# Attention by random features with two feed-forward layers: values by features a slot later, and the first casts on GpSimd

## Chip, cores and metric

The kernel runs on one core of a Trainium2 chip. The metric is the time on the device in microseconds, as the median of three runs. The profile is of one execution of its own.

## What is computed

Attention with positive random features, then a gated feed-forward layer, then one with h cos(h):

```python
def phi(x):
    proj = np.einsum('bhsd,md->bhsm', x, omega)
    h = proj - np.sum(x * x, axis=-1, keepdims=True) / 2.0
    return np.exp(h - np.max(h, axis=-1, keepdims=True)) / np.sqrt(m)
q_p, k_p = (phi(q_s), phi(k_s))          # q, k scaled by D ** -0.25
kv = np.einsum('bhsm,bhsd->bhmd', k_p, v)
z = np.sum(k_p, axis=2)
x = einsum(q_p, kv) / (einsum(q_p, z) + 1e-06)
xn = x / rms(x) * rms_g
g = xn @ w_gate
y = (silu(g) * (xn @ w_val)) @ w_out
h = y @ w_in
out = (h * np.cos(h)) @ w_out2
```

There are 4 batches, 8 heads, 576 positions of 64, and 128 features; so 2304 tokens of 512. The inner widths are 1536 and 2048. All is float32.

## The kernel before

The tokens are cut into 18 tiles of 128, of keys and of queries. The attention starts in 24 slots. In each slot one tile, of keys or of queries, is projected on the features (`project`, TensorE, two banks of the ring of four "w" banks), reduced to its maxima (`features`, L435, VectorE) and exponentiated (L437, ScalarE, eight instructions). Slots 0 to 5 are key tiles 0 to 5; then queries 0 to 5 stand in slots 6, 9, 12, 15, 20 and 23, and keys in the others (the last in 21 and 22). The older tiles of queries take further steps in later slots: transposing their features, sums and quotients, the square, its root on GpSimd, the norm (`norm`, L494), turning (`turn`, one "w" bank) and splitting into two parts (`put`, L516 and L518). A key tile's features are multiplied with its values in `kv_product` (L591) one slot after it was projected; tiles 4 and 13 lie in two batches and take two. The values of the tile three later are loaded one slot behind that.

The order is written out by hand: every engine runs its instructions in the order of the program, slot by slot, and within a slot by the line of `older` steps with `begin` in it. The norm comes ahead of the projection, the values by features last.

Between the slots the weights are made ready, 512 columns at a time (a chunk): they come packed, are unpacked by integer operations and split into an upper and a lower part. `wts.tick(n)` does n steps of the generator `run` at the end of a slot. `front` is the unpacking: shift L190 on VectorE (reads W, which `exponent` made on ScalarE), L193 for every third chunk, L195, the `exponent` of the next chunk, L204 on VectorE, L209 on GpSimd. `early_back` of the chunk before is woven in, a step each behind the first two: `high` (L214, a cast on ScalarE, followed by the DMA issue L170 of a chunk three later) and `low` (L217, GpSimd). So step 8c of the count is L190 of chunk c, 8c+1 `high` of chunk c-1, 8c+3 its `low`, 8c+4 L195, 8c+5 the exponent of chunk c+1, 8c+6 L204 and 8c+7 L209. W has one buffer. 25 steps lie in slots 1 to 5, 8 in slots 6 to 13, and 36 in slots 14 to 22.

Behind the slots come 24 steps of the first products (two half steps each; a product and a part of L886), among which the other 12 tiles of queries and the later steps of the weights (`wts.pace`) lie. The rest is products of the later groups and the second layer.

Of the kernel before, what the change touches and what calls it, by code (L numbers as in the profile page):

```python
# [33 lines left out]
F32 = mybir.dt.float32  # L34
# [10 lines left out]
P = 128  # L45
NB = 384
# [10 lines left out]
def attention_then_ffn(ctx: ExitStack, tc: tile.TileContext, qT, kT, v, omT, wc1, rms_g, wc2, out, B, H, S, D):  # L57
    nc = tc.nc
    M = omT.shape[1]
    DM = H * D  # L60
    KD = DM // P
    HP = H // 2
# [21 lines left out]
    def parts(t):  # L84

        pr, i = divmod(t, TPP)
        if i == MIX:
            return [(2 * pr, 0, P // 2), (2 * pr + 1, P // 2, P // 2)]
        return [(2 * pr + (i > MIX), 0, P)]
# [37 lines left out]
    class Weights:  # L127
# [83 lines left out]
            yield  # L211

        def high(self, src, t, to):
            nc.scalar.copy(t[:, 0, to], src)  # L214

        def low(self, src, t, to):
            nc.gpsimd.tensor_tensor(t[:, 1, to], src, f32(t[:, 0, to]), op=ALU.subtract)  # L217
# [184 lines left out]
    wts = Weights()  # L402
# [144 lines left out]
    with tc.manual_schedule():  # L547
        fp = ctx.enter_context(tc.tile_pool(name="fp", bufs=2, reuse_waits="tile"))
        early = ExitStack()
        ap = early.enter_context(tc.tile_pool(name="att", bufs=2, side="right", reuse_waits="tile"))  # L550
        depth = {"gain": 1, "raw": 3, "feat": 3, "mx": 6, "den": 4}
        with_keys = {"raw": 1, "feat": 2}
        turn_of = {"raw": 0, "feat": 0}
        keys = [True]

        def att_tile(what, shape, dt, name):
            own = depth.get(what, 2)
            if keys[0] and what in with_keys:
                n = turn_of[what] % (own + with_keys[what])
                turn_of[what] += 1  # L560
                if n >= own:
                    return vp.tile(shape, dt, tag=what, name=name, bufs=with_keys[what])
            return ap.tile(shape, dt, tag=what, name=name, bufs=own)

        kv = [ap.tile([P, KVW], F32, name=f"kv{b}", bufs=1) for b in range(B)]
        NV = 3
        values = ExitStack()
        vp = values.enter_context(tc.tile_pool(name="values", bufs=1, side="right", reuse_waits="tile"))
        vt = [vp.tile([P, H, D + 1], F32, name=f"v{i}", bufs=1) for i in range(NV)]
        att = Attention(att_tile, "q", kv)  # L570


        acc = {}

        def load_v(t):
            if t < NTILE:
                nc.sync.dma_start(vt[t % NV][:, :, 0:D], v[t])

        def kv_product(t, i):
# [3 lines left out]
            for r in range(2):  # L583
# [3 lines left out]
                for h in range(HP):  # L587
                    hh = 2 * h + r
                    for c in range(2):
                        half_c = slice(c * M // 2, (c + 1) * M // 2)  # L590
                        nc.tensor.matmul(  # L591
                            acc[b, r][half_c, h * P:h * P + D + 1], att.e["k", t, r][p0:p0 + n, h, half_c],
                            vt[t % NV][p0:p0 + n, hh, :],
                            start=begin and h == 0, stop=end, skip_group_check=True)
# [24 lines left out]
        def combinations(p):  # L619
# [27 lines left out]
            for kk in range(2):  # L647
# [19 lines left out]
                less(s3, s3, s1)  # L667
                yield from [None] * (5 if few else 1)
                high(s1)
                yield  # L670
                if few:
                    high(s2)
                    yield from [None] * 4
                lower(s1)
                yield
                if not few:
                    high(s2)
                    yield
# [64 lines left out]
        SLOTS = len(tiles)  # L743
# [3 lines left out]
        begins, then = {}, {}  # L747
        for s, (nm, t) in tiles.items():
            if nm == "k":
                for i in range(len(parts(t))):  # L750
                    then.setdefault(s + 1 + i, []).append((1, kv_product, t, i))
                then.setdefault(s + 2 + i, []).append((0, load_v, t + NV))
            else:
                for i in range(1, 8):
                    at = s + i + (s >= SLOTS - 1 or i > 1)
                    then.setdefault(at, []).append((-i, query_step, t, i))
# [6 lines left out]
        def load_ahead(s):  # L763
            at = order.index(s) if s in tiles else -1
            if at >= 0 and at + AHEAD[0] < len(order) and at + AHEAD[0] not in asked:
                asked.add(at + AHEAD[0])
                att.load(*tiles[order[at + AHEAD[0]]])

        def older(s, *steps):
            for step in steps:  # L770
                for k, f, *args in then.get(s, []):
                    if k == step:
                        f(*args)

        def begin(s):
            if s in tiles:
                att.project(*tiles[s])
                for r in range(2):
                    att.features(*tiles[s], r)
# [21 lines left out]

        for s in range(SLOTS):
            load_ahead(s)
            if s in (0, 1):
                load_v(s + 1)
                wts.load(s + 1, nc.sync)
            if s == 3:
                att.load_gain()
            older(s, 0, -5)
            begin(s)  # L810
            older(s, -7, -6, -4, -3, -1, -2, 1)
            if s:
                wts.tick(5 if s < 6 else 1 if s < 14 else 4 if s + 1 < SLOTS else 0)


        att.tag = "w"
# [48 lines left out]
        def silu(blk, f, ps):  # L865
            a = row(F32, f"gv{blk}_{f}")
            nc.scalar.activation(a, ps, AF.Silu)
            return a
# [82 lines left out]
        for n, (g, blk, f, first, last) in enumerate(steps):  # L951
# [9 lines left out]
            s = SLOTS + 2 * n  # L961
# [3 lines left out]
            a = silu(blk, f, ps)  # L965
# [466 lines left out]
```

## Time and profile before

| | |
|---|---|
| time, median of three runs | 957.8 us (956.14 to 958.7) |
| the profiled execution's own time | 955.29 us |
| its span | 953.5 us |
| TensorE busy | 929.5 us, 97% |
| VectorE busy | 713.4 us, 75% |
| ScalarE busy | 537.1 us, 56% |
| GpSimd busy | 415.5 us, 44% |

The span in 40 slices of 23.8 us, each digit the busy share in tenths; PEclk is the granted clock of TensorE in tenths of full speed:

```profile
PE   8988999999999999999999999999999999999998
DVE  5797777878854685585876658996799787786766
ACT  7898776756535443435363645664655565464443
PEclk9999999989999999999999999999999999999999
```

PE is TensorE, PEld its loading of weights, DVE VectorE, ACT ScalarE, POOL GpSimd, SP SyncE. A line of a timeline gives the start, the duration, the engine, the line of the program, the operation, out<-in, and in brackets how long the engine idled before it and what ended that. Instructions of one engine overlap a little, so what one costs its queue is read from the start of the next rather than from its duration.

### The profile page before, as it was taken

The page shows a single profiled execution, that of the slowest core. Times are in us where ns is not written, and L with a number is a line of the kernel's source. Part 1 is how long each engine was busy: PE and PEld are TensorE (multiplying, and loading weights), DVE is VectorE, ACT ScalarE, POOL GpSimd, SP SyncE. Part 2 cuts the span into 40 slices and gives each one's busy share as a digit, 9 for nine tenths or more (in the row PEclk, how much of TensorE's full clock was granted, in tenths as well). Part 3 has the DMA queues.
Part 4 walks back from the last instruction along what each step waited for, and adds up shares of the span by engine and source line. Part 5 has one row for each costly group of instructions (what it writes and reads, how often), then busy time and mean ns, then how long its engine had stood idle before and what let it go on. Part 6 is the DMA issues. An engine that isn't in the chain of part 4 may idle for free. (4 is left out here: it accounts for less than half of the span.)

```text
span 953.5 us, 17373 instructions
## 1 busy us (share of the span) xinstructions
PE 929.5 (97%) x6337; PEld 866.7 (91%) x6337; DVE 713.4 (75%) x1159; ACT 537.1 (56%) x1155; POOL 415.5 (44%) x377
## 2 busy tenths in 40 slices
PE   8988999999999999999999999999999999999998
PEld 7777998989999999999999998889888988988997
DVE  5797777878854685585876658996799787786766
ACT  7898776756535443435363645664655565464443
POOL 2143387467836975376583763320343220240000
PEclk9999999989999999999999999999999999999999
DMA  9774378777796988766989693967622767307554
GB/s 290 201 192 164 134 264 292 264 257 271 231 346 226 400 288 294 268 200 202 386 297 383 231 374 130 355 211 251 210 93 101 251 205 285 124 21 282 191 227 160
DMA packets 112214, 227.71 MB, mean 239 GB/s; under 512 B 28160, under 2 KB 63616, under 8 KB 112128
## 3 DMA queue, kind: packets, MB, share of 16 engines
q1 hardware_dynamic: 110832, 222.34, 67.5%
q10 hardware_dynamic: 1296, 4.26, 1.4%
q8 instruction: 50, 0.82, 0.4%
q14 instruction: 36, 0.29, 0.1%
HBM read 156.04 MB, written 70.52 MB: 238 GB/s over the span
## 5 line engine op out<-in xcount | busy, mean ns | idle before, releaser
L1253 PE MATMUL o_ps<-w,o 128*128 128x512 f32 x864 | 226.0, 393 | 0.7 <-DVE o L1056 0.7
L209 POOL TENSOR_TENSOR f<-f,raw 128x512 f32<-128x512 f32 x68 | 94.4, 1388 | 229.2 <-DVE raw L204 199.2
L1253 PEld LDWEIGHTS o_ps<-w,o 128*128 128x128 f32 x864 | 159.7, 188 | 24.5 <-DVE o L1056 1.1
L217 POOL TENSOR_TENSOR w<-b,w 128x512 fp32r<-128x512 f32 x88 | 115.5, 1318 | 137.0 <-ACT w L214 113.7
L833 PE MATMUL gv_ps<-xhl,w 128*128 128x384 f32 x576 | 109.3, 338 | 1.3 <-DVE eT L454 1.1
L833 PEld LDWEIGHTS gv_ps<-xhl,w 128*128 128x128 f32 x576 | 101.6, 190 | 2.4 <-DVE eT L454 1.6
L1152 PE MATMUL y<-t,w 128*128 128x384 f32 x576 | 102.0, 334 | 0.3 <-POOL w L217 0.3
L1152 PEld LDWEIGHTS y<-t,w 128*128 128x128 f32 x576 | 100.0, 188 | 0.6 <-POOL w L217 0.6
L1053 ACT CAST o<-turns 128x384 fp32r<-128x384 f32 x96 | 47.4, 513 | 93.4 <-DVE turns L1234 93.4
L1045 PE MATMUL Xh<-T,w 128*128 128x384 f32 x432 | 87.4, 336 | 1.6 <-ACT h L1198 1.6
L1045 PEld LDWEIGHTS Xh<-T,w 128*128 128x128 f32 x432 | 76.8, 188 | 9.7 <-ACT h L1198 4.1
L1045 PE MATMUL X<-T,w 128*128 128x384 f32 x432 | 80.7, 334 | 0.0
L1045 PEld LDWEIGHTS X<-T,w 128*128 128x128 f32 x432 | 75.4, 188 | 0.0
L214 ACT CAST w<-b 128x512 fp32r<-128x512 f32 x88 | 50.5, 580 | 31.9 <-DVE b L274 24.8
L1056 DVE TENSOR_TENSOR o<-turns,o 128x384 fp32r<-128x384 f32 x96 | 60.0, 639 | 8.5 <-ACT o L1053 8.1
L886 PE MATMUL y_ps<-t,w 128*128 128x384 f32 x288 | 61.8, 350 | 0.3 <-ACT t L873 0.3
L1019 ACT ACTIVATE turns<-turns,half_pi 128x768 f32<-128x768 f32 (+1 forms) x50 | 45.7, 914 | 22.8 <-DVE turns L1223 22.7
L1045 PE MATMUL Yh<-B,w 128*128 128x384 f32 x288 | 58.0, 336 | 0.0
L1223 DVE SCALAR_TENSOR_TENSOR turns<-turns,r 128x768 f32<-128x768 int32 (+1 forms) x50 | 56.4, 1128 | 1.7
L1234 DVE TENSOR_TENSOR turns<-h,turns 128x768 f32<-128x768 f32 (+1 forms) x50 | 55.1, 1101 | 2.5 <-ACT turns L1019 2.5
L190 DVE TENSOR_SCALAR f<-W 128x512 int32<-128x512 int32 x68 | 44.0, 647 | 15.1 <-ACT W L182 6.5
L1045 PEld LDWEIGHTS Yh<-B,w 128*128 128x128 f32 x288 | 51.4, 188 | 4.2 <-ACT h L1198 0.4
(116 smaller groups left out, 1804.6 us busy)
## 6 DMA issues: line engine op xcount, KB each, us to landing
T<-T_dram SPq DMA_DIRECT2D x48, 768.0 KB, 7.1
raw<-wc SPq DMA_DIRECT2D x60, 512.0 KB, 5.1
B<-yh_dram SPq DMA_DIRECT2D x21, 768.0 KB, 5.5
kept<-f SPq DMA_DIRECT2D x56, 256.0 KB, 5.1
b<-kept SPq DMA_DIRECT2D x56, 256.0 KB, 4.8
B<-x_dram SPq DMA_DIRECT2D x15, 768.0 KB, 6.7
x_dram<-xhl SPq DMA_DIRECT2D x12, 768.0 KB, 5.7
s<-x_dram SPq DMA_DIRECT2D x24, 384.0 KB, 5.6
```

What stands on the lines that cost most here:

```text
L209: nc.gpsimd.tensor_tensor(f32(f), f32(f), rest, op=ALU.add)
L214: nc.scalar.copy(t[:, 0, to], src)
L217: nc.gpsimd.tensor_tensor(t[:, 1, to], src, f32(t[:, 0, to]), op=ALU.subtract)
L833: nc.tensor.matmul(o, w[i], x[j], start=n == 0, stop=n == len(terms) - 1)
L886: nc.tensor.matmul(yacc[blk][e], w[:, i, e * P:(e + 1) * P], t[:, j], start=first and i + j == 0, stop=last and j == 1)
L1045: nc.tensor.matmul(o, w[:, i, c + kk * P:c + (kk + 1) * P], x[:, j, kk], start=begin and n == 0, stop=n == 5, skip_group_check=True)
L1053: nc.scalar.copy(t[:, 0], a)
L1056: engine.tensor_tensor(t[:, 1], a, f32(t[:, 0]), op=ALU.subtract)
L1152: nc.tensor.matmul(acc[e], w[:, i, e * P:(e + 1) * P], t[:, j], start=f == fs[0] and i + j == 0, stop=f == fs[-1] and j == 1)
L1223: nc.vector.scalar_tensor_tensor(r, a, -TWO_PI_LO, b, op0=ALU.mult, op1=ALU.add)
L1234: at(mu, lambda: nc.vector.tensor_tensor(r, h, r, op=ALU.mult))
L1253: nc.tensor.matmul(oacc[blk][j], o[:, x, js], w[:, y], start=first and n == 0, stop=last and n == 2)
```

## The change

In the first slots the values are multiplied with the features two slots behind the projection instead of one, and at the latest in slot 23. There are four buffers of values instead of three; the fourth is first loaded in slot 2, and each later load stands a slot later. The features of the slots have eight buffers instead of five, three of them borrowed from the rows of the products. The weights take 4 steps instead of 5 in slots 1 to 5 and 2 instead of 1 in slots 6 to 13, which makes 72 instead of 69. While `early` holds (in the slots), `high` is a copy on GpSimd instead of ScalarE. The load of the gains goes from slot 3 to slot 8.

```diff
         def high(self, src, t, to):
-            nc.scalar.copy(t[:, 0, to], src)
+            if self.early:
+                nc.gpsimd.tensor_copy(t[:, 0, to], src)
+            else:
+                nc.scalar.copy(t[:, 0, to], src)
...
-        with_keys = {"raw": 1, "feat": 2}
+        with_keys, vp_bufs = {"raw": 1, "feat": 5}, {"raw": 1, "feat": 2}
...
+                if n >= own + vp_bufs[what]:
+                    a = fp.tile([P, 2, NB], F32, tag="t", name=name, bufs=3).rearrange("p a c -> p (a c)")
+                    return a[:, 0:HP * M].rearrange("p (h m) -> p h m", m=M)
                 if n >= own:
-                    return vp.tile(shape, dt, tag=what, name=name, bufs=with_keys[what])
+                    return vp.tile(shape, dt, tag=what, name=name, bufs=vp_bufs[what])
...
-        NV = 3
+        NV = 4
...
                 for i in range(len(parts(t))):
-                    then.setdefault(s + 1 + i, []).append((1, kv_product, t, i))
-                then.setdefault(s + 2 + i, []).append((0, load_v, t + NV))
+                    then.setdefault(min(s + 2 + i, SLOTS - 1), []).append((1, kv_product, t, i))
+                then.setdefault(s + 3 + i, []).append((0, load_v, t + NV))
...
             load_ahead(s)
+            if s == 2:
+                load_v(3)
...
-            if s == 3:
+            if s == 8:
                 att.load_gain()
...
-                wts.tick(5 if s < 6 else 1 if s < 14 else 4 if s + 1 < SLOTS else 0)
+                wts.tick(4 if s < 6 else 2 if s < 14 else 4 if s + 1 < SLOTS else 0)
```

## Rows read from the trace of the kernel before

**Rows 1.** Timeline of TensorE, around slot 23 and at 200 us.
```profile
78.94 1.16 PE L426 MATMUL qp_ps<-om,qraw 64*128 64x128 f32 x14 [1.65 <-ACT ke L437]
...
81.00 1.10 PE L591 MATMUL kv_ps<-v,ke 128*64 128x65 f32 x32
82.04 4.43 PE L833 MATMUL gv_ps<-xhl,w 128*128 128x384 f32 x24
...
200.32 0.46 PE L426 MATMUL qp_ps<-om,qraw 64*128 64x128 f32 x2 [1.76 <-issue]
```
**Rows 2.** ScalarE's lines, 7:82 us: busy, mean ns | idle before, its end.
```profile
L437 ACT ACTIVATE ke<-kp_ps,kmx 128x128 f32<-128x128 f32 x144 | 39.4, 407 | 7.7 <-DVE kmx L435 7.7
...
L214 ACT CAST w<-f 128x512 fp32r<-128x512 f32 x8 | 5.2, 645 | 2.8 <-POOL f L209 2.8
```
**Rows 3.** Timeline of VectorE, from the reductions of slot 14 to slot 22.
```profile
47.60 1.29 DVE L435 TENSOR_REDUCE kmx<-kp_ps 128x4 f32<-128x512 f32 x2 [1.09 <-ACT ke L437]
48.80 0.75 DVE L518 TENSOR_TENSOR xhl<-xT_ps,xhl 128x256 fp32r<-128x256 f32 x2
49.47 0.42 DVE L195 TENSOR_SCALAR raw<-f 128x512 int32<-128x512 int32 x1
49.80 0.75 DVE L494 SCALAR_TENSOR_TENSOR x<-x,ms,gain 128x512 f32<-128x512 f32 x1
50.67 1.29 DVE L435 TENSOR_REDUCE qmx<-qp_ps 128x4 f32<-128x512 f32 x2
51.88 0.15 DVE L476 TENSOR_SCALAR den<-num_ps 128x4 f32<-128x4 f32 x1
...
53.36 0.68 DVE L204 SCALAR_TENSOR_TENSOR raw<-raw 128x512 f32<-128x512 uint32 x1
53.95 0.42 DVE L190 TENSOR_SCALAR f<-W 128x512 int32<-128x512 int32 x1
...
55.49 0.68 DVE L454 COPY eT<-eT_ps 128x512 f32<-128x512 f32 x1
56.09 0.68 DVE L193 SCALAR_TENSOR_TENSOR f<-W,f 128x512 int32<-128x512 int32 x1
56.80 1.38 DVE L195 TENSOR_SCALAR raw<-f 128x512 int32<-128x512 int32 x1
...
61.06 1.78 DVE L494 SCALAR_TENSOR_TENSOR x<-x,ms,gain 128x512 f32<-128x512 f32 x1
...
71.70 1.61 DVE L494 SCALAR_TENSOR_TENSOR x<-x,ms,gain 128x512 f32<-128x512 f32 x1
...
75.96 1.27 DVE L435 TENSOR_REDUCE kmx<-kp_ps 128x4 f32<-128x512 f32 x2
```
**Rows 4.** Timeline of ScalarE, slots 13 to 15.
```profile
47.36 0.70 ACT L516 CAST xhl<-xT_ps 128x256 fp32r<-128x256 f32 x2
...
49.20 0.62 ACT L214 CAST w<-f 128x512 fp32r<-128x512 f32 x1
49.72 2.18 ACT L437 ACTIVATE ke<-kp_ps,kmx 128x128 f32<-128x128 f32 x8
51.73 0.74 ACT L184 ACTIVATE W<-raw 128x512 f32<-128x512 f32 x1
52.30 2.24 ACT L437 ACTIVATE qe<-qp_ps,qmx 128x128 f32<-128x128 f32 x8
```
**Rows 5.** GpSimd's casts at line L638, whole span: duration in ns, min/median/max.
```profile
L638 POOL CAST s<-s x16: 496/696/1046, 129.2 to 251.4; 128x384 fp32r<-128x384 f32 x16
```
**Rows 6.** Timeline of GpSimd, beside the norm of 61.06 us.
```profile
60.89 1.41 POOL L209 TENSOR_TENSOR f<-f,raw 128x512 f32<-128x512 f32 x1 [0.57 <-DVE raw L204]
```
**Rows 7.** Timeline of VectorE, L190 in slot 5 and at 199 us.
```profile
24.60 0.79 DVE L190 TENSOR_SCALAR f<-W 128x512 int32<-128x512 int32 x1 [0.87 <-ACT W L182]
...
199.13 0.43 DVE L190 TENSOR_SCALAR f<-W 128x512 int32<-128x512 int32 x1 [3.60 <-ACT W L184]
```
**Rows 8.** A stretch: us, busy (count) of PE, PEld, DVE, ACT, POOL, granted clock, DMA.
```profile
200.00:208.00 8.00, 7.25 (x32) 6.87 (x33) 6.84 (x11) 5.43 (x13) 7.68 (x8) 0.57 0.50 181
```

## The prediction

> **What bounds the kernel now.** I read the slices of the page first: TensorE is busy in nearly all of the 953.5 us except at the start, so only a stage in which TensorE has gaps can pay. The change touches the first 24 slots, from 4 us to the first product at 82.04 us [rows 1]. There I read the waits and the lines of ScalarE, then the timelines of ScalarE and VectorE side by side. ScalarE loses 7.7 us waiting for the reductions of VectorE, and 2.8 us in four of its eight casts L214, which wait for GpSimd's L209 [rows 2]. VectorE shows the opposite: from 47.60 us each of its instructions begins where the one before ends, slot after slot, and so with few breaks to 78 us [rows 3]. So in slots 14 to 22 the last wait to end is VectorE's queue; ScalarE is second, TensorE third.
>
> **How the slots hang together.** Every engine runs in program order. Slot s projects on TensorE, reduces on VectorE (L435), exponentiates on ScalarE (L437), does the older steps, and then the steps of the weights. A chunk has eight steps: shift L190 on VectorE, cast L214 and load of a later chunk, L193 (every third chunk), L217 on GpSimd, L195, the next chunk's exponent (ScalarE), L204, L209 on GpSimd. L190 needs the exponent. From the starts of neighbours [rows 3, 4]: reductions 1.2, exponentials 2.01, exponent 0.57 (its own 0.74), L214 0.52, put(0) with square and copy 1.84, L204 0.59, L190 0.42, L193 0.71, L195 0.33, quotients 1.48, L518 0.67, L454 0.60, norm 0.75.
>
> **Part by part.**
>
> The cast: eight of the twelve first chunks reach L214 in the slots. ScalarE loses 8 x 0.52 = 4.2 us of work and the 2.8 us of waits. The DMA issue behind the cast stays on ScalarE and needs the same L209 (its buffer), but now stands a slot behind it, so the wait isn't inherited. ScalarE isn't what ends last, so I cost this at 0; its cover is VectorE's queue, and if that cover were gone it would be worth up to 7.
>
> GpSimd gets eight casts of 128x512. The nearest row casts 128x384 in 0.50 to 1.05 us, median 0.70 [rows 5]; by width 0.66 to 1.39, I take 0.93, in all 7.4 us. They are not late for any reader: low follows them in the same queue. They hold VectorE up, though: the norm takes 1.78 instead of 0.75 when it meets L209, another 1.61, and L195 1.38 instead of 0.43 [rows 3, 6]. These are 1.03 + 0.86 + 0.95 = 2.8 us in slots 14 to 22, beside ten GpSimd instructions of about 1.41, 14.1 us. With four casts more it is, at that rate, 2.8 x 17.8/14.1 = 3.6 us for the changed kernel; the other end is 0, since GpSimd no longer waits for ScalarE and may finish while VectorE itself waits. I take 1.8, the middle.
>
> The Trainium skill speaks against this part (SBUF — State Buffer, Who interferes with whom): VectorE and GpSimd share a port pair as an exclusive lock, and the later one blocks for the whole instruction. The long norms agree. By that rule alone eight casts could cost 8 x 0.93 = 7.4 us.
>
> The step count: this is the term that decides. With 5 and 1 steps, step 37 (the exponent of chunk 5) was the last of slot 14, and its L190 the third step of slot 15. With 4 and 2, 36 steps are done before slot 14, and every even slot from 14 on does exponent, L204, L209, L190 in this order. So L190 waits for an exponent that stands behind this slot's exponentials, and the next slot's reductions stand behind L190, ScalarE behind those. An even slot, reduction to reduction, becomes 0.65 (first reduction) + 2.01 + 0.74 + 0.42 = 3.8 us. It is 4.6 in slots 14 and 20 (the norm follows L190) and 3.8 + 1.84 = 5.7 in slot 16, whose put(0), square and copy stand ahead of the exponent. The odd ones stay as VectorE makes them: slot 15 1.2 + 1.48 + 0.71 + 0.33 = 3.7; 17 1.2 + 0.67 + 0.33 + 0.75 = 2.95; 21 1.2 + 0.60 + 0.71 + 0.33 = 2.8. Slot 19 is set by the bank that the projection of slot 20 waits for: 0.65 + 1.0 (half of the exponentials) + 1.16 [rows 1] + 0.1 = 2.9. The eight from 14 to 21 sum to 31.1, against 75.96 - 47.60 = 28.4 before [rows 3]: +2.7. The trace of before shows this wait once, in slot 5, where exponent and L190 fell into one slot: L190 stood 0.87 us [rows 7].
>
> The same alignment comes in slots 2 and 4, while fewer steps lie in slots 1 to 5 and eight more in 6 to 13. Worked in the same way these stretches come out even at slot 14 (49.65 against 49.72 for the exponentials); bounds -1 and +1.5.
>
> Values by features a slot later: TensorE no longer stands before the 1.04 us of L591 until ScalarE is done, but the projection behind it needs a bank that the same exponentials release, so little is gained; 0 to -1 in slots 2 to 5, inside the bounds above. At the end the last two key tiles both fall into slot 23: TensorE, which waited 1.65 us there before its projection and did one L591 group of 1.04 us [rows 1], does two behind the same wait: +1.0 ahead of the first product.
>
> Fourth buffer, buffers of features, gain: SyncE issues the same loads in the same order; the load of the fourth values waits for nothing, and gain goes five slots later and is first read in slot 12. Three feature buffers lie in the product rows, which nothing else uses before slot 24. 0, hidden under the slots, at most one issue of about 0.5 us.
>
> Sum for the slots: 2.7 + 1.0 + 1.8 = +5.5, bounds +2 and +8.
>
> Behind the slots: 72 instead of 69 steps are done, so each later step comes up to three earlier. In the kernel before, the exponent of chunk 22 and its L190 fall into one half step; L190 stands 3.60 us, L518 and L872 stand behind it, TensorE waits 1.76 us for their banks, and its granted clock is then 0.57 over 8 us [rows 1, 7, 8]: the level of 1.2 GHz for most of it, 0.43 x 7.25 us busy = 3.1 us lost. Three steps earlier the two lie in different half steps. Without that stall some 1.4 of the 1.76 us go (L872's bank would still come a little late, an estimate) and the 3.1 of clock: -4.5. Two other pairs now share a half step (chunks 15 and 25) and could do the same, so the other end is 0. I take the middle, -2.2.
>
> **Sum.** +5.5 - 2.2 = +3.3 us. The profiled execution is 955.3 with a span of 953.5, 2.5 below the median; a difference carries over unchanged, since behind 90 us TensorE is busy nearly throughout (the slices again): 957.8 + 3.3 = 961.1.
>
> **Rivals.**
> *Faster, by the alignment behind the slots.* The stall at 199 us goes whole (-4.5) and no pair takes its place, while the slots cost under 1.5 us, because GpSimd finishes under VectorE's waits (0 for contention) and the missing casts let the exponent come earlier than I count. For it: L190 after L204 often met a finished exponent in before. Against: the chain reduction, exponentials, exponent, L190 has no slack in even slots. It decides where the first product starts before 83.5 us. 957.8 - 3.5 = 954.3.
> *Slower, by the clock.* With 5 us more in the last slots TensorE idles up to 3 us at a time around slots 16 and 20. A gap of 1.65 us before slot 23 left the granted clock at full (the slices of the page); one of 1.76 us at 200 us was followed by 0.57 [rows 1, 8]. If it falls there, projections, sums and the first products take twice as long, and one such stretch costs up to 3.1 us more: about 964 to 965. By the Trainium skill (TensorE: Matmul & The Clock Gate, Part 1: The HAM clock gate) the low level is what an engine without recent work gets; this trace agrees at 200 us only.
> *Nothing that can be measured*, because the steps are re-ordered by slack that I don't see: 957.8.
>
> **How the numbers follow.** The forecast has 0.50; its own range is 957.5 to 964.5 (slots +2 to +8, behind them -4.5 to 0, not both ends at once), of which 0.20 lies within 0.3% (2.9 us, about what a measurement of this kernel can tell from no change) and 0.30 above. Faster by alignment 0.30 (0.27 below, 0.03 within), clock 0.15, nothing 0.05. So faster 0.27, same 0.28, slower 0.45. The range takes in most of the rivals: 951.5 to 966.
>
> **What would show it.** Right: in even slots from 14 VectorE waits at L190 for the exponent, 1 to 3 us each, longest in slot 16; ScalarE waits for L435 right after; first product at 85 to 89 us; two L591 groups ahead of it; no 3.6 us wait near 200 us. Wrong: first product at or before 82 us, L190 without waits, or ScalarE busy without a break in the slots. Then ScalarE was the bound after all and its 4 to 7 us come through, and the forecast's sign is wrong.

## The result and the profile after

The changed kernel takes 969.3 us (median of four runs, 965.82 to 971.72) against 957.0 us for the kernel before beside it (954.85 to 958.7): a ratio of 1.0127, interval 1.0085 to 1.017. It is slower by 12.4 us, where I had forecast 3.3; 969.3 lies above the range. The profiled execution is the quickest of the four (965.8 us, span 964.0 against 953.5), so the trace shows 10.5 of the 12.4 us.

The page of the changed kernel, its slices (tenths busy, as before):

```profile
span 964.0 us, 17342 instructions
...
PE   8969999999999999999999999999999999999998
...
DVE  4877778888953696577684758986889787786766
ACT  5867776776433534355443646564656564454443
...
PEclk8989999999999999999999999999999999999999
```

Most of the loss is made in the first four slices: ScalarE and VectorE are less busy there than before in the first and the third (for ScalarE in part because its eight casts, 5.2 us [rows 2], are gone), TensorE in the third (6 instead of 8 tenths). VectorE's timeline of the changed kernel (start, duration, in brackets the idle time and what ended it) at the shift L190 and at the reductions that open slots 14, 15 and 22 (L438 was L435):

```profile
16.05 0.72 DVE L190 TENSOR_SCALAR f<-W 128x512 int32<-128x512 int32 x1 [1.60 <-ACT W L182]
22.23 1.54 DVE L190 TENSOR_SCALAR f<-W 128x512 int32<-128x512 int32 x1 [2.13 <-ACT W L184]
...
49.93 1.29 DVE L438 TENSOR_REDUCE kmx<-kp_ps 128x4 f32<-128x512 f32 x2 [0.75 <-ACT ke L440]
54.31 0.50 DVE L190 TENSOR_SCALAR f<-W 128x512 int32<-128x512 int32 x1 [1.83 <-ACT W L184]
54.73 1.75 DVE L497 SCALAR_TENSOR_TENSOR x<-x,ms,gain 128x512 f32<-128x512 f32 x1
56.40 1.28 DVE L438 TENSOR_REDUCE qmx<-qp_ps 128x4 f32<-128x512 f32 x2
65.39 0.54 DVE L190 TENSOR_SCALAR f<-W 128x512 int32<-128x512 int32 x1 [2.78 <-ACT W L182]
80.61 0.57 DVE L190 TENSOR_SCALAR f<-W 128x512 int32<-128x512 int32 x1 [1.11 <-ACT W L184]
84.97 1.28 DVE L438 TENSOR_REDUCE kmx<-kp_ps 128x4 f32<-128x512 f32 x2
89.02 0.43 DVE L190 TENSOR_SCALAR f<-W 128x512 int32<-128x512 int32 x1 [2.17 <-ACT W L182]
```

The unbroken queue of [rows 3] now has a hole in slots 14, 16, 20 and 22 where L190 waits for the exponent; slot 18 alone has none. TensorE of the changed kernel, same columns (L597 was L591, L429 L426, L841 L833):

```profile
29.15 2.23 PE L597 MATMUL kv_ps<-v,ke 64*64 64x65 f32 x64
...
67.94 2.04 PE L429 MATMUL kp_ps<-om,kraw 64*128 64x128 f32 x14 [4.37 <-DVE xhl L521]
...
86.88 1.16 PE L429 MATMUL qp_ps<-om,qraw 64*128 64x128 f32 x14 [1.34 <-DVE raw L204]
88.95 2.04 PE L597 MATMUL kv_ps<-v,ke 128*64 128x65 f32 x64
90.91 4.44 PE L841 MATMUL gv_ps<-xhl,w 128*128 128x384 f32 x24
...
258.15 0.66 PE L507 MATMUL xT_ps<-ident,x 128*128 128x128 f32 x4 [2.11 <-ACT gv L875]
...
643.64 1.32 PE L1053 MATMUL Xh<-T,w 128*128 128x384 f32 x6 [1.40 <-ACT h L1206]
```

The first product stands at 90.91 instead of 82.04 [rows 1]: +8.88. This delay is still +8.73 at the start of the 13th step of the products; at the 15th it is +5.16, because the stall at 199 us [rows 7] is gone; at the end of the steps it is +9.1 again, because of the new gap at 258.15, and at the end of the span +10.54. The windows show the clock (us, busy and count by engine, granted clock, DMA share, GB/s); the kernel before had 1.00 in the first three and 0.72 in the fourth:

```profile
10.00:20.00 10.00, 8.11 (x136) 6.86 (x136) 6.60 (x12) 7.06 (x26) 3.22 (x3) 0.84 1.12 293
20.00:30.00 10.00, 9.63 (x146) 8.30 (x146) 7.83 (x14) 7.71 (x29) 4.53 (x5) 0.82 0.89 260
60.00:70.00 10.00, 5.01 (x66) 4.30 (x67) 6.38 (x13) 6.65 (x22) 3.90 (x5) 0.73 0.43 125
196.00:208.00 12.00, 11.47 (x105) 10.75 (x104) 10.95 (x22) 8.73 (x20) 4.89 (x5) 1.00 0.93 317
256.00:264.00 8.00, 5.89 (x27) 5.85 (x27) 7.28 (x11) 3.19 (x8) 7.73 (x8) 0.79 0.67 218
```

### The profile page after: what moved, and what is told of

The parts are those of the page before. It is cut to its first block, busy times and chain, and to the rows that moved or that the text cites. A ratio compares the mean times of both kernels' runs of the same rounds, so it can differ in the third digit from the quotient of the medians.

```text
span 964.0 us, 17342 instructions
## 1 busy us (share of the span) xinstructions
PE 931.1 (97%) x6337; PEld 869.0 (90%) x6337; DVE 715.3 (74%) x1160; ACT 531.9 (55%) x1147; POOL 419.1 (43%) x385
## 5 line engine op out<-in xcount | busy, mean ns | idle before, releaser
L841 PE MATMUL gv_ps<-xhl,w 128*128 128x384 f32 x576 | 109.2, 338 | 2.0 <-DVE den L479 1.0
L841 PEld LDWEIGHTS gv_ps<-xhl,w 128*128 128x128 f32 x576 | 101.5, 190 | 3.2 <-issue 1.6
L1053 PEld LDWEIGHTS Xh<-T,w 128*128 128x128 f32 x432 | 76.8, 188 | 10.5 <-ACT h L1206 4.8
L217 ACT CAST w<-b 128x512 fp32r<-128x512 f32 x88 | 50.5, 580 | 32.8 <-DVE b L277 25.7
L190 DVE TENSOR_SCALAR f<-W 128x512 int32<-128x512 int32 x68 | 47.0, 692 | 23.6 <-ACT W L182 12.4
L204 DVE SCALAR_TENSOR_TENSOR raw<-raw 128x512 f32<-128x512 uint32 x68 | 54.8, 806 | 0.5
```

The lines of the kernel that those rows point to most:

```text
L204: nc.vector.scalar_tensor_tensor(rest, raw[:, :, 0].bitcast(U32), 2.0 ** -52, rest, op0=ALU.mult, op1=ALU.mult)
L841: nc.tensor.matmul(o, w[i], x[j], start=n == 0, stop=n == len(terms) - 1)
L1053: nc.tensor.matmul(o, w[:, i, c + kk * P:c + (kk + 1) * P], x[:, j, kk], start=begin and n == 0, stop=n == 5, skip_group_check=True)
```

## The experiments

**The step count alone, and a shift of it.** steps_only has the new counts and nothing else; before_36_steps leaves slots 1 to 5 alone and reaches the same 36 steps by three more in slot 13.

```diff
-                wts.tick(5 if s < 6 else 1 if s < 14 else 4 if s + 1 < SLOTS else 0)
+                wts.tick(4 if s < 6 else 2 if s < 14 else 4 if s + 1 < SLOTS else 0)   # steps_only
+                wts.tick(5 if s < 6 else 1 if s < 13 else 4 if s + 1 < SLOTS else 0)   # before_36_steps
```

> The kernel before with the new step counts alone (4 and 2 instead of 5 and 1). Theory A (alignment: the exponent and its L190 fall into one slot, and the reductions stand behind L190): L190 waits 1 to 3 us in slots 2, 4, 14, 16, 20 and 22 as in the changed kernel, the first product comes at 87 to 91 us, the time is 7 to 13 us over before. Theory C (the casts on GpSimd hold VectorE up): no cast is moved here, so within 2 us of before. Theory K (values a slot later leave TensorE idle and its clock falls): values are not moved here, so no stretch of half clock in the first 82 us and within 2 us of before.

Measured: 964.7 us, ratio 1.0105 (1.0085 to 1.0125); first product 88.37 (+6.33).

> The kernel before with three more steps in slot 13 (36 done ahead of slot 14, 5 and 1 otherwise): in slots 14 to 22 the phase of the changed kernel, in slots 1 to 12 that of before. Theory A: the L190 waits come in slots 14, 16, 20 and 22 alone; the first product 4 to 7 us later than in before; time 4 to 9 us over before, or up to 4 less where the half clock at 200 us goes. Theories C and K: within 2 us of before.

Measured: 965.2 us, 1.0105 (1.0087 to 1.0123); first product 89.17 (+7.13). So 36 steps ahead of slot 14 cost as much as all of the new counts; what slots 1 to 5 do makes no difference that the intervals show. Both kernels have 72 steps done at the first product instead of 69, as the changed one has; what that costs without the alignment is measured below (before_72). VectorE and TensorE of steps_only:

```profile
51.84 0.43 DVE L190 TENSOR_SCALAR f<-W 128x512 int32<-128x512 int32 x1 [1.84 <-ACT W L184]
61.85 0.43 DVE L190 TENSOR_SCALAR f<-W 128x512 int32<-128x512 int32 x1 [2.79 <-ACT W L182]
77.73 1.38 DVE L190 TENSOR_SCALAR f<-W 128x512 int32<-128x512 int32 x1 [0.85 <-ACT W L184]
...
67.19 1.92 PE L591 MATMUL kv_ps<-v,ke 64*64 64x65 f32 x32
69.03 1.16 PE L426 MATMUL kp_ps<-om,kraw 64*128 64x128 f32 x16
```

From reduction to reduction, slots 14 to 21 take (us):

| slot | 14 | 15 | 16 | 17 | 18 | 19 | 20 | 21 | sum |
|---|---|---|---|---|---|---|---|---|---|
| worked out | 4.6 | 3.7 | 5.7 | 2.95 | 3.8 | 2.9 | 4.6 | 2.8 | 31.1 |
| steps_only | 5.40 | 3.74 | 5.60 | 3.07 | 5.17 | 3.63 | 5.63 | 2.85 | 35.1 |
| changed kernel | 6.47 | 3.74 | 5.71 | 3.78 | 4.20 | 3.14 | 5.15 | 2.85 | 35.0 |

Slots 15, 16 and 21 are as worked out. In 14 the exponentials begin 1.6 us behind the reduction instead of 0.65, since ScalarE is late there. In 18 nothing waits at L190: VectorE's own queue is the longer chain, with the quotients and a copy of the finished sums of the values (L602) that the working had left out; it takes 4.29 at full clock (steps_filler below). On top the values by features run at the half clock (1.92 instead of about 1.1), and the two copies wait 0.23 and 0.36 us for them. In 20 L190 takes 1.38 instead of 0.42.

**One and two steps instead of three.**

```diff
+                wts.tick(5 if s < 6 else 1 if s < 13 else 2 if s < 14 else 4 if s + 1 < SLOTS else 0)   # 34; with 3: 35
```

> The kernel before with one more step of the weights in slot 13 (34 instead of 33 before slot 14). Theory (what costs is that the exponent and the L190 that reads it fall into one slot, not the number of steps): with 34 the exponent is the third step of an even slot and L190 the second of the next, the reductions of a slot between them, so no wait of over 1 us at L190 in slots 14 to 22, first product 81 to 83.5, median within 3 us of before, though before_36_steps, two steps on, cost 9.7. Rival (each step moved ahead of slot 14 costs its own time, some 3 us): first product 84 to 85, median 957.5 to 960.

Measured: 957.2 us, 1.0022 (1.0009 to 1.0034); first product 84.18.

> The kernel before with two more steps of the weights in slot 13 (35 before slot 14). Theory: the exponent is the second step of an even slot and L190 the first of the next, directly ahead of that slot's work but still behind the exponentials of one slot only; the wait is short (under 1 us), first product 81.5 to 84.5, median within 4 us of before. Rival (each step costs its own time): first product 86 to 87.5, median 960 to 963. If 34 or 35 comes out below before by more than 2 us, it beats both kernels.

Measured: 960.7 us, 1.0056 (1.0037 to 1.0074); first product 86.64. Neither idea is right alone: the waits at L190 are gone in both, as the theory wants (at most 0.47 us from slot 14 on), but the first product is as late as the rival said. The rows show another collision. First L204 on VectorE and `low` on GpSimd of before_34_steps, then the norm of before_35_steps with GpSimd's instructions around it:

```profile
51.08 1.80 DVE L204 SCALAR_TENSOR_TENSOR raw<-raw 128x512 f32<-128x512 uint32 x1
51.05 1.28 POOL L217 TENSOR_TENSOR w<-f,w 128x512 fp32r<-128x512 f32 x1 [0.30 <-ACT w L214]
```
```profile
53.05 1.77 DVE L494 SCALAR_TENSOR_TENSOR x<-x,ms,gain 128x512 f32<-128x512 f32 x1 [0.72 <-POOL ms L490]
50.50 1.27 POOL L217 TENSOR_TENSOR w<-f,w 128x512 fp32r<-128x512 f32 x1 [8.73 <-ACT w L214]
51.86 0.51 POOL L489 TENSOR_SCALAR ms<-ms 128x1 f32<-128x1 f32 x1
52.98 1.29 POOL L209 TENSOR_TENSOR f<-f,raw 128x512 f32<-128x512 f32 x1
```

L204 takes 1.80 instead of 0.68 beside L217; with 35 the root that the norm needs also stands behind L217. The price climbs, in the ratios 0.2, 0.6 and 1.05% for 34, 35 and 36 steps, and only the last one has the long waits at L190. It isn't the price of the phase alone (of which step falls into which slot): with these counts 70, 71 and 72 steps are done at the first product, and one or three steps more in slot 23, with the phase untouched, cost 0.2 and 0.42% (before_70 and before_72 below). By these medians the phase is worth some 0.6% at 36 steps and nothing that can be told at 34.

**The change with the alignment taken out.** all_but_steps is the changed kernel with the old counts (the diff above reversed), after_33_steps with 33 steps ahead of slot 14 in another split:

```diff
-                wts.tick(4 if s < 6 else 2 if s < 14 else 4 if s + 1 < SLOTS else 0)
+                wts.tick(4 if s < 6 else 2 if s < 11 else 1 if s < 14 else 4 if s + 1 < SLOTS else 0)
```

> The changed kernel with the old step counts (5 and 1). Theory A: no L190 wait in slots 14 to 22; the first product at 80 to 84 us; time 953 to 960. Theory C: eight casts stay on GpSimd, so 5 to 12 us over before remain. Theory K: the values stay a slot later, the half clock at 17 us stays, and most of the 12 us too.

Measured: 962.1 us, 1.0077 (1.0057 to 1.0096); no wait at L190 in slots 14 to 22, and still the first product at 91.60.

> The changed kernel with 33 instead of 36 steps done ahead of slot 14 (4, then 2 to slot 10, then 1): the phase of before in slots 14 to 22, everything else as changed. Theory A: the first product 4 to 7 us earlier than in the changed kernel (84 to 87 us), L190 waits only in slots 2 and 4; time 958 to 964. Theory C: casts as in the changed kernel, so 966 to 972 stays. Theory K: 966 to 972 stays, with half clock at 17 and 65 us.

Measured: 962.2 us, 1.0064 (1.0043 to 1.0085); first product 89.03. The new counts are thus worth 5 to 6 us in the changed kernel: the alignment together with three steps more at the first product, since both runs have 69 there. And 6 to 7 us stay that I had not counted. From slot 22 to the first product both take 8.44 us against 6.08 before: here the two groups of L591 in slot 23 do cost, part of them at the half clock (3.19 us in all_but_steps).

**The other two parts alone.** casts_only is the kernel before with `high` on GpSimd in the slots; values_only the changed kernel with the old counts and the cast back on ScalarE, so only the values' order, their buffers and the gain's load, which no run takes apart.

> The kernel before with the eight early casts on GpSimd alone. Theory C (casts hold VectorE up): first product 3 to 8 us later than in before, VectorE's own instructions (L190, L195, L204, L494) longer by that sum, time 959 to 965. Theory K (the values a slot later are what costs 6.6 us with the old steps): first product within 1.5 us of before, no half clock in the first 82 us, time 952 to 958.

Measured: 956.9 us, 1.0019 (1.0006 to 1.0032), that is +1.8 us: the value taken. In its profile the first product is at 84.97, 2.93 later than before, between what the two theories say; slots 14 to 21 take 0.9 of that, and there is half clock in the ten us from 10, from 60 and from 80 us (0.83 in each). In the changed kernel eight casts took 5.0 us on GpSimd, less than the 7.4 I had worked out (the mean is 629 ns):

```profile
L215 POOL CAST w<-f 128x512 fp32r<-128x512 f32 x8 | 5.0, 629 | 0.5
```

> The kernel before with the values a slot later, the buffers and the gains, but with old steps and the casts on ScalarE. Theory K: half clock in the slots as in the run with all but the steps, the pile of 64 L591 matmuls in slot 7 ahead of a projection, first product 5 to 10 us later than in before, time 959 to 965. Theory C: first product within 2 us of before, time 953 to 959.

Measured: 962.1 us, 1.0068 (1.0047 to 1.0089), +6.5 us at the ratio: this is the part that I had put at 0 to -1. TensorE and VectorE of values_only in slot 7, and the window of it:

```profile
26.48 2.19 PE L444 MATMUL eT_ps<-ident,qe 128*128 128x128 f32 x8 [1.40 <-ACT qe L437]
28.60 3.93 PE L594 MATMUL kv_ps<-v,ke 64*64 64x65 f32 x64
32.46 1.71 PE L426 MATMUL kp_ps<-om,kraw 64*128 64x128 f32 x16
...
34.21 1.29 DVE L435 TENSOR_REDUCE kmx<-kp_ps 128x4 f32<-128x512 f32 x2 [5.21 <-PE kp_ps L426]
...
26.00:34.00 8.00, 7.52 (x88) 6.53 (x90) 2.99 (x6) 4.68 (x17) 1.03 (x1) 0.57 0.62 194
```

and of the kernel before, the same work:

```profile
22.72 2.23 PE L591 MATMUL kv_ps<-v,ke 64*64 64x65 f32 x64
25.63 1.16 PE L426 MATMUL kp_ps<-om,kraw 64*128 64x128 f32 x16 [0.68 <-issue]
26.73 1.86 PE L444 MATMUL eT_ps<-ident,qe 128*128 128x128 f32 x8
28.52 1.16 PE L426 MATMUL kp_ps<-om,kraw 64*128 64x128 f32 x16
```

Key tile 4 lies in two batches; its second part and tile 5 were both due in slot 6, where 2.23 us fitted ahead of a projection that waited anyway. A slot later they stand in slot 7, behind the eight transposes of query 0 and ahead of slot 8's projection. On top the granted clock is half there, so the pile takes 3.93 us, and VectorE waits 5.21. The move does take a wait away: L591 of the kernel before waited 0.96 and 0.64 us for loads of values (at 13.85 and 17.61 us), here and in the changed kernel none does.

**Pile or clock?** values_two_parts leaves tiles 4 and 13 in their old slots; values_filler adds 24 spare matmuls to TensorE in slots 1 to 7.

```diff
-                    then.setdefault(min(s + 2 + i, SLOTS - 1), []).append((1, kv_product, t, i))
+                    then.setdefault(min(s + (1 if len(parts(t)) > 1 else 2) + i, SLOTS - 1), []).append((1, kv_product, t, i))
```
```diff
+        def warm(n):
+            for _ in range(n):
+                nc.tensor.matmul(ps[:, 0:P], ident, ident, start=True, stop=True)
...
+            if s == 7:
+                warm(6)
             older(s, -7, -6, -4, -3, -1, -2, 1)
+            if 1 <= s < 7:
+                warm(3)
```

> As values_only, but the two key tiles that lie in two batches keep their old slots, so 64 L591 matmuls no longer stand between the transposes of slot 7 and the projection of slot 8. Theory P (the pile): the exponentials of slot 8 begin within 1.5 us of before instead of 4.5 later, and the first product 3 to 5 us earlier than in values_only (85 to 87 us); time 956 to 960. Theory K (the clock falls because the first slots lack the values' work): the half clock at 10 and 27 us stays and with it most of the delay; 960 to 963.

Measured: 958.8 us, 1.0043 (1.0027 to 1.0059); first product 86.43 instead of 90.16.

> As values_only, with spare matmuls of the identity on an unused bank behind the values of slots 1 to 6 (three each) and behind the projection of slot 7 (six), 24 in all, some 0.3 us each at most. Theory K: the granted clock stays full to 33 us, the 64 matmuls of slot 7 take 2.2 instead of 3.9 us, the exponentials of slot 8 begin 2 to 3 us earlier than in values_only; first product 86 to 88 us, time 957 to 960. Theory P: the pile at full clock still stands there, 1.5 to 2.5 us remain at slot 8; time 960 to 962.

Measured: 957.4 us, 1.0033 (1.002 to 1.0046); first product 85.14. Its TensorE and the same window:

```profile
28.43 2.23 PE L594 MATMUL kv_ps<-v,ke 64*64 64x65 f32 x64
...
26.00:34.00 8.00, 8.00 (x164) 7.46 (x166) 5.19 (x11) 6.08 (x23) 1.02 (x1) 1.00 0.76 228
```

More work on TensorE makes the kernel about 3.3 us quicker (0.35 points of the ratio): the granted clock stays full in the first slots, the pile included. Each remedy takes away a third to a half. The two aren't independent, though: without the pile the half clock at 27 us is gone too (0.97 from 20 to 30 us, half from about 17 to 20.5 us only), and the interval of values_two_parts overlaps that of values_only. So the clock's part is shown, and what the pile costs at a given clock isn't.

**The same filler in the changed kernel.**

> The changed kernel with 24 spare identity matmuls in slots 1 to 7 (three behind the values of each of slots 1 to 6, six behind the projection's predecessors in slot 7), as in values_filler; nothing else changed. It computes the same result and does more work on TensorE. Theory (the fall of the granted clock in the first slots is part of the price): the half-clock stretch from 16.9 us goes, the slots up to 14 shorten, first product 87.5 to 88.5 instead of 90.91, median 963 to 966 instead of 969.3; the half-clock stretch at 64.7 us stays, since the waits at L190 are still there, and so a price of 7 to 9 us over before. Rival (the clock falls because the slots wait, and costs nothing beyond the waits): first product 90.5 to 91.5, median 968 to 971.

Measured: 969.5 us, 1.0136 (1.0113 to 1.016); in the profile the first product is at 95.03, in a run that has half clock again from 67.0 to 73.8 and 87.5 to 94.3 us. My theory failed here, and not by this one profile: the five runs had a mean granted clock of 0.991 to 0.995, the changed kernel's four 0.983 to 0.990, and the time is the same. The half clock at 16.9 us does go, but slot 14 begins at 50.67 against 49.93: slots 2 to 5 of the changed kernel wait at L190 (rows above), which a faster TensorE doesn't shorten, and its pile at 29.15 had run at full clock (2.23) without help.

> The changed kernel with 33 steps before slot 14 as in the kernel before (4 in slots 1 to 5, 2 in 6 to 10, 1 in 11 to 13), which takes the L190 waits out of the even slots, and the 24 spare matmuls, which keep TensorE's clock: both suspected causes taken away at once, with values later, buffers, gain and GpSimd casts left in. Theory (alignment, pile with clock, and contention are the three prices): no L190 waits in slots 14 to 22, no half clock before 70 us, first product 84.5 to 86.5, median 957 to 960, within 0.3% of before. Rival (a fourth cause that neither removes): first product 88 to 90, median 961 to 963 as after_33_steps.

Measured: 961.0 us, 1.0055 (1.0036 to 1.0074), against 1.0064 without filler: no difference that the intervals show, and again a miss: the first product at 88.89 and the time are the rival's. With the alignment out of slots 14 to 22 (slots 2 and 4 keep waits of 1.61 and 2.14 us at L190) and the clock up to 53.9 us full, 0.55% stays, close to casts_only and values_filler together (0.19 + 0.33%). In the profile 2.4 of the 6.9 us to the first product lie behind slot 22's reduction (8.44 against 6.08), where the two groups of L591 take 3.02 us, part of it at half clock.

**Does the clock make the chain long?** steps_only with spare matmuls ahead of the projections of slots 14 to 22.

```diff
+                nc.tensor.matmul(ps[:, D + 2:P], ident, ident[:, D + 2:P], start=False, stop=False, skip_group_check=True)
...
+            if 14 <= s < SLOTS - 1 and acc:
+                warm(list(acc.values())[0], 6 if s < 16 else 10)
             begin(s)
```

> steps_only with spare matmuls on TensorE ahead of the projections of slots 14 to 22 (six or ten of 62 columns, added into columns of the values' bank that nothing reads), placed where TensorE waits for VectorE's reads of the banks. The result is the same, the work more. The question is why the chain of slots 14 to 21 took 35.1 us in steps_only (47.45 to 82.54) where I had worked out 31.1. Theory A (the waits at L190 let TensorE's granted clock fall to half, 58.6 to 62.1, 65.5 to 68.9 and 82.5 to 85.9 us, and the long L591 and projections hold slots 18 to 20): with the clock kept, the chain takes 32 to 33.5 us, first product 85.5 to 87, median 960 to 962.5. Theory B (ScalarE and contention make the waits longer, the clock only follows): chain 34.5 to 35.5, first product 88 to 89, median 964 to 966.

Measured: 965.7 us, 1.0118 (1.0094 to 1.0141); first product 90.18. Windows 58 to 72 us of steps_only, then of steps_filler, and a stretch of the latter's TensorE:

```profile
58.00:72.00 14.00, 11.94 (x184) 10.82 (x186) 10.34 (x24) 10.05 (x34) 4.71 (x5) 0.76 0.40 113
```
```profile
58.00:72.00 14.00, 14.00 (x240) 13.06 (x239) 10.35 (x25) 10.07 (x33) 4.80 (x6) 1.00 0.49 133
...
72.75 2.44 PE L804 MATMUL kv_ps<-ident 128*128 128x62 f32 x20
75.13 1.16 PE L426 MATMUL qp_ps<-om,qraw 64*128 64x128 f32 x16
```

The clock is kept, the loss isn't undone: the chain of slots 14 to 21 takes 36.65 us, longer than either theory had it. The run doesn't separate the two cleanly: slots 14, 18 and 20 fall from 5.40, 5.17 and 5.63 to 5.01, 4.29 and 4.79, near what I had worked out, but ten spare matmuls last 2.4 us and themselves delay the projections of the slots between. That the clock adds some 2 us to the chain is argued from these three slots, not shown. Of its six runs four kept a granted clock of 0.996 or more and took 964.3 to 966.2 us, where steps_only, at 0.991 to 0.996, took 963.5 to 968.2.

**Behind the slots.** before_72 is the kernel before with three steps in slot 23, before_70 with one.

```diff
+                wts.tick(5 if s < 6 else 1 if s < 14 else 4 if s + 1 < SLOTS else 3)   # before_72; with 1: before_70
```

> The kernel before with three more steps in slot 23, so 72 done at the first product as in the changed kernel while slots 1 to 22 are untouched. Theory A2 (the shift behind the slots takes one stall and gives another): first product within 0.7 us of before, TensorE's gap at 200 us and its half clock gone (-3.5), and a new gap near 250 us, where ScalarE waits for a row that a store of y holds (+3); time within 2 us of before. Rival: no new gap, 951 to 953.

Measured: 958.2 us, 1.0042 (1.0027 to 1.0057). In its profile the stall at 199 us is gone and the 15th step starts 3.69 us earlier than before; then comes TensorE's

```profile
249.41 0.66 PE L504 MATMUL xT_ps<-ident,x 128*128 128x128 f32 x4 [2.20 <-ACT gv L867]
```

and at the end of the steps 1.2 of the 3.7 us are left. So both gaps are as Theory A2 has them, but the time isn't: it is 4.0 us over before by the ratio, and the profile (the quickest of six, span 954.4) shows only 0.9 of it, 2.1 us lost behind the steps. The changed kernel has the same gap 9 us later (258.15). What its ScalarE waits for there:

```profile
257.61 0.49 ACT L875 ACTIVATE gv<-gv_ps 128x384 f32<-128x384 f32 x1 [3.11 <-DMA y_dram<-y]
```

> The kernel before with one more step in slot 23. Worked from the step count only one pair of exponent and L190 that stands ahead of a projection's bank is left behind the slots instead of four: first product within 0.5 us of before, no gap at 200 us; if no other row or bank wait takes its place 951 to 954, else 954 to 957.

Measured: 956.2 us, 1.002 (1.0007 to 1.0033): no stall at 200 us, but gaps of 1.45, 1.46 and 2.43 us at 214, 220 and 252 us. One step or three, the stall moves. The first product is at 84.19, not within 0.5 us of before: the granted clock is 0.84 from 20 to 30 us and 0.83 from 80 to 90 us, in stretches where it was 1.00 in the kernel before. Slots 1 to 22 have the same instructions in both; in slot 4 TensorE waited 1.95 us for a load of values, in the kernel before 0.64. before_72, also unchanged in these slots, has 0.83 from 10 to 20 us. So a first product read from one profile can be some 2 us late for reasons that aren't the edit's; the 6.3 and 7.1 us of the 36 steps are well beyond that, the 2.1 with 34 steps and the 2.9 of casts_only aren't.

## Why the prediction was right or wrong

**Term by term.** In the profiles slots 0 to 13 came out at +2.3 us (forecast 0, at most 1.5), slots 14 to 21 at +6.7 (2.7 for the alignment and 1.8 for the casts), slot 22 to the first product at -0.1 (+1.0), and what lies behind at +1.7 (-2.2): +10.5 against +3.3. All but one were too low, the term behind the slots by most. The median is 1.9 us higher than this profile shows.

**Direction and main mechanism: right.** With 36 steps the exponent and its L190 fall into one even slot, L190 waits 1 to 3 us from slot 14 on, longest in slot 16, and VectorE's wait becomes everybody's; steps_only and before_36_steps show it alone (of their 1.05%, 0.42 is what before_72 pays for the three steps without the alignment). At 90.91 the first product lies beyond the 85 to 89 that I had named.

**The size of the alignment: +2.7 worked out, +6.7 measured** (49.93 to 84.97 against 47.60 to 75.96 [rows 3]). The failing step was to take ScalarE as free when an even slot's reduction is done, the chain through L190 as the longer one in every even slot, and every other duration as in the kernel before. With ScalarE late (slot 14), VectorE's own queue longer than the chain (slot 18, 4.29 against 3.8), VectorE's L190 and norm meeting GpSimd (slots 14 and 20; some of the separate 1.8 us of contention is in this figure) and the values at half clock (slot 18), slots 14, 18, 19 and 20 came out 0.7 to 1.4 us longer in steps_only; in the changed kernel slot 14 is 1.9 longer, 1.0 of it the norm of 1.75.

**Values a slot later: 0 to -1 forecast, +6.5 measured alone.** This step is simply wrong. I looked at the bank that the next projection waits for, but not at where the move puts the groups of L591 that are due two at a time: from slot 6 to slot 7 and from 19 to 20, beside other work of TensorE's. Of the doubled groups I counted the one in slot 23 alone. In the changed kernel slots 1 to 13 end 2.3 us late instead of even, beyond the bound of 1.5. The doubled group in slot 23 is there (2.04 us at 88.95), yet from slot 22 to the first product the kernels are level (5.94 against 6.08), so its +1.0 was covered there. Where the slots don't wait at L190 it wasn't: 8.11 in values_only and 8.44 in all_but_steps and after_33_steps, with half clock in that stretch (before_70, with half clock there and a single group, takes 7.40), and 6.55 in values_filler with the clock full.

**The clock: chance 0.15, the place slots 16 to 20.** It came in the first slots too (0.84 and 0.82 in the windows from 10 to 30 us), after idle times of under 1 us each, where I had reasoned that a gap of 1.65 us had done no harm. In values_only it costs 3 us of 6.5. Nor does it need the change: before_70 and before_72 have it in one stretch of these slots each, with the instructions of the kernel before. By the Trainium skill (TensorE: Matmul & The Clock Gate, Part 1: The HAM clock gate) an engine without recent work gets the low level; values_filler agrees: with work of no use the granted clock was 1.00 where it had been 0.57. In the changed kernel the same filler gave nothing back (after_filler).

**The cast: right, in part by luck.** +1.8 forecast, +1.8 measured; but 1.8 was the middle of 0 and 3.6, and the interval goes from 0.6 to 3.1. The rule of the Trainium skill (SBUF — State Buffer, Who interferes with whom) would have made it up to 7.4; two norms (1.76 and 1.78 us) and two L195 (1.38 and 1.54) of slots 14 to 22 in casts_only show the blocking, together 4.1 us above their own time where the kernel before had 2.8, so 1.3 us of the possible 7.4 (5.0 with the casts as they were measured).

**Behind the slots: -2.2 forecast, +1.7 in the profiles.** The stall at 199 us went, as said, and with it 3.6 us; the gap at 258 us took 3.9 back, and gaps like the one at 643.64 us the rest. The failing step was to end the range at 0, with other pairs doing the same. What happened lies beyond it, by another releaser: a row buffer held by a store. before_72, the three steps without the change in the slots, costs 4.0 us in all. I had searched the steps for pairs of exponent and L190, and not asked what TensorE, earlier by 3 us, would meet next.

The parts don't add: 1.05 + 0.68 + 0.19 is 1.9%, measured 1.27%. One piece of it can be read: the pile of slot 7 ran at full clock in the changed kernel (2.23 us against 3.93), and slot 8 begins its reductions at 32.51, in values_only at 34.21, the same 1.7 us. Another is the doubled group in slot 23, above. What stays open is the rest of that difference, the clock's share of the chain, and why the granted clock falls in one execution and not in another of the same instructions. The granted clock goes with the 6 us between single runs of the changed kernel: 965.8 and 967.5 us had a mean granted clock of 0.990 and 0.989, 971.2 and 971.7 had 0.983 and 0.986; that it is the cause isn't shown.

## What to carry to other kernels

When work is dealt out in fixed steps between fixed slots, it matters where a producer and its reader fall against the slot's own work, and not only how many steps there are: write out, for each slot, the order of every engine, and count a moved step in the slot that it comes into, beside what stands there. A stall removed in the middle of a tightly buffered stage is only worth what the next buffer leaves of it; look for the next one before booking the gain.

## What the runs showed of the hardware

Spare matmuls made a kernel quicker: 24 of them, 0.94 us for a group of three, took values_only from 1.0068 to 1.0033 by keeping the granted clock at 1.00 where it had been 0.57; in the changed kernel the same 24 gave nothing (1.0136 against 1.0127). The granted clock fell to half in the first slots of before_70 and before_72 (0.84 from 20 to 30 us, 0.83 from 10 to 20 us) and not in the kernel before, with the same instructions there. And VectorE's instruction over 128x512 took 1.75 to 1.80 instead of 0.68 to 0.75 us beside one of GpSimd, for L204 as for the norm, and 1.38 instead of 0.42 for L190.
